# Attention with an exact top-32 and a mixture of experts: the selection's table of counts in PSUM, and the offset's bf16 source as three padded rows

## The chip, the core and the metric

The kernel is one program on one core of a Trainium2 chip. Its metric is the device time of one execution in microseconds, and lower is better. The core has a TensorE for matrix products (PE; its weight loads, PEld, are listed apart), a VectorE (DVE), a ScalarE (ACT), a GpSimd (POOL) and a queue engine (SP) that issues most of the transfers. SBUF is the on-chip working memory. PSUM, eight banks of 2 KB a partition, is where TensorE writes.

## The reference

```python
def _attn_ref(q, k, v):                       # 8 batches, 8 heads, 576 positions, 64 wide
    scores = scale * np.matmul(q, k.transpose(0, 1, 3, 2))
    kth = np.partition(scores, -top_k, axis=-1)[..., -top_k:-top_k + 1]     # top_k = 32
    mask = scores >= kth
    scores = np.where(mask, scores, -1000000000.0)
    ...softmax over each row...
    return np.matmul(attn, v)

def _moe_ref(x, expert_emb, tau, w1, w2):     # 4608 tokens of 512, 8 experts of 1024
    logits = xn @ en.T / tau                  # rows of x and of expert_emb, normalized
    expert_idx = np.argmax(logits, axis=1)
    out[mask] = gate_w[mask, None] * (np.maximum(x[mask] @ w1[e], 0.0) @ w2[e])
```

Each row of scores keeps its 32 largest entries before the softmax. The result goes through one expert per token, with the gate's probability as its weight.

## The kernel before, in words

The work falls into two stages. The first is the attention, with part of the expert work threaded through it; the second is the rest of the experts. The change touches the first alone.

The attention runs over 32 head units: a unit is one head of two batches (`NU` = 32). A unit has nine score tiles of 128 query rows by 576 keys (the last 64 rows of both batches share a tile), so there are 288 tiles. One loop (lines 919 to 1094) writes the program out step by step. Step i takes up a new tile on every engine, each engine at another point of the pipeline, and each engine runs its instructions in just this order. For one tile j the points are:

- step j-2: TensorE computes the scores into `sc` (`nat`, line 184), ScalarE copies them to SBUF as `xs` (line 663);
- steps j and j+1: VectorE finds the top eight of each of eight groups (line 670) and merges them (lines 680 to 686). The merge gives the maximum and a lower bound on the threshold;
- step j+2: ScalarE counts with a Sign how many scores lie under that bound (line 692), GpSimd multiplies `xs` with the signs (`y`, line 698), so that VectorE can find the next eight values below the bound;
- step j+3: VectorE takes these eight (line 706). Then comes the **select** (line 707): a table `win` of 18 constants is compared with the count, the entry that fits is multiplied with the sorted values, and the sum is the 32nd largest value, `tall`;
- step j+4: ScalarE makes the second Sign, `s2`, against `tall` (line 714);
- step j+5: VectorE makes the **offset** `r` = max(s2 x 2^60, row maximum), bf16 in and out (line 720). TensorE subtracts it from the recomputed, transposed scores (line 752), so that everything outside the top 32 vanishes in the exponential (line 753).

Nine steps after a unit's first tile its output begins. In each step TensorE runs the scores of tile i+2, then a **chunk** (transposed scores and offsets of 128 keys, line 752), then the **AV matmuls** (line 767) that multiply the weights of an earlier chunk with the values and accumulate in the PSUM tile `po`, and at times a segment of expert work (lines 422 and 431). Two of the nine steps of a unit are longer on TensorE: one has a chunk for both batches, one has two AV groups. Twice in a unit ScalarE copies the finished sums out of `po` to `ob` (line 785).

On VectorE a step's order is: the offset of tile i-5; then, interleaved, the groups of tile i, the merge of tile i-1, and at the end the maximum (line 706) and the select of tile i-3. All of the eight PSUM banks are taken: one for the expert work, two for `sc`, one for `po`, four for the chunks. `po` is 512 columns wide; the AV matmuls use the first 365.

The framework that builds the program puts in the waits, and keeps track of reads and writes by tile: an instruction that reads a tile waits for its last writer, and a writer for its last readers. It does this for the whole tile, whatever columns are used; for a PSUM tile it orders the reads of two engines too.

Of the kernel before, what the change touches and what calls it, by code (L numbers as in the profile page):

```python
# [12 lines left out]
BF16 = mybir.dt.bfloat16  # L13
I32 = mybir.dt.int32
AF = mybir.ActivationFunctionType
# [5 lines left out]
B, H, S, D = 8, 8, 576, 64  # L21
N, DM, E, F = B * S, H * D, 8, 1024
P = 128
# [25 lines left out]
def attn_moe_kernel(ctx: ExitStack, tc: tile.TileContext, qk, vb, vt, emb, tau, w1, w2, out):  # L49
    nc = tc.nc  # L50
# [27 lines left out]
    win = consts.tile([P, 9, 2], F32, name="win", tag="win")  # L78
# [448 lines left out]
    with ExitStack() as sx:  # L527
        bk = sx.enter_context(tc.tile_pool(name="bk", bufs=1, side="right"))
        wk = sx.enter_context(tc.tile_pool(name="wk", bufs=2, side="right"))
# [10 lines left out]
        tall = wa.tile([P, NU * 9], F32, name="tall", tag="tall", bufs=1)  # L540
        call = wa.tile([P, NU * 9], F32, name="call", tag="call", bufs=1)
        sc = ps_s.tile([P, 2, 512], F32, name="sc", tag="sc")
        po = ps_s.tile([P, 512], F32, name="po", tag="po")
# [2 lines left out]
                             start=(n == 0), stop=(n == WU - 1))  # L546
        pov = po[:, 0:5 * VW].rearrange("p (t e) -> p t e", t=5)

        NV = 2
        vts = []  # L550
        for i in range(NV):
# [102 lines left out]
        xss, cas, zs, s1s, y2s, s2s, cnt1 = ({} for _ in range(7))  # L654
# [46 lines left out]
        def select(i):  # L701
            z = zs.pop(i)
            y2, c1 = y2s.pop(i), cnt1.pop(i)
            jk = wa.tile([P, 9, 2], F32, name=f"jk{i}", tag="jk", bufs=2)
            return [
                lambda: nc.vector.max(out=z[:, 16:24], in_=y2),  # L706
                lambda: nc.vector.scalar_tensor_tensor(  # L707
                    jk, win, c1, z[:, 15:24, None].to_broadcast([P, 9, 2]),
                    op0=ALU.is_equal, op1=ALU.mult, accum_out=tall[:, i:i + 1]),
            ]  # L710

        def sign2(i):
            s2 = wk.tile([P, S], BF16, name=f"s2_{i}", tag="s2", bufs=2)
            nc.scalar.activation(s2, xss.pop(i), AF.Sign, bias=tall[:, i:i + 1], scale=-1.0,  # L714
                                 accum_out=call[:, i:i + 1])
            s2s[i] = s2

        def offset(i):
            r = wk.tile([P, S], BF16, name=f"r{i}", tag="r", bufs=14)
# [198 lines left out]
        i = -1  # L918
        while i < ntile + 12 or sideq or later or bankq or early or squares or wq or mo["seg"] \
# [87 lines left out]
            for u, b in norms:  # L1007
                if u % H == 0:
                    for j in ((0, 2), (1,))[b]:
                        xt[u // H][0][j] = xp.tile([P, (4, 4, 1)[j], DM], F32,  # L1010
                                                   name=f"x{u // H}_{j}", tag=f"x{j}",
                                                   bufs=1 + (j > 0))
# [32 lines left out]
            if i == ntile + 4:  # L1045
                nc.vector.tensor_scalar(tall, tall, TMIN, 0.0, op0=ALU.is_lt, op1=ALU.add,
                                        accum_out=bad[:, 0:1])
# [5 lines left out]
                                        accum_out=bad[:, 2:3])  # L1053
# [43 lines left out]
    with mx:  # L1097
        wl = mx.enter_context(tc.tile_pool(name="wl", bufs=1, reuse_waits="tile"))
        wk = mx.enter_context(tc.tile_pool(name="mwk", bufs=1, reuse_waits="tile"))
# [475 lines left out]
```

## Time and profile before

| | |
|---|---|
| three runs, us | 1456.82, 1464.04, 1464.93 (median 1464.04) |
| the profiled execution, us | 1470.54 |
| its span, first to last instruction, us | 1468.8 |
| busy share of the span | PE 91%, VectorE 81%, ScalarE 68%, GpSimd 55% |
| mean granted TensorE clock | 0.955 of full speed |
| first and last select (line 707) begin, us | 23.1 and 1042.7 |

The attention stage thus takes about 1020 us of the span, and 287 steps lie between the two selects. A busy share over the whole span hides that the engines' loads differ between the stages, so the views below are cut at 1044 us. "Idle before, releaser" in the groups says how long the engine stood idle directly in front of a group's instructions, and what ended that.

### The profile page before, as it was taken

The page shows a single profiled execution, that of the slowest core. Times are in us where ns is not written, and L with a number is a line of the kernel's source. Part 1 is how long each engine was busy: PE and PEld are TensorE (multiplying, and loading weights), DVE is VectorE, ACT ScalarE, POOL GpSimd, SP SyncE. Part 2 cuts the span into 40 slices and gives each one's busy share as a digit, 9 for nine tenths or more (in the row PEclk, how much of TensorE's full clock was granted, in tenths as well). Part 3 has the DMA queues.
Part 4 walks back from the last instruction along what each step waited for, and adds up shares of the span by engine and source line. Part 5 has one row for each costly group of instructions (what it writes and reads, how often), then busy time and mean ns, then how long its engine had stood idle before and what let it go on. Part 6 is the DMA issues. An engine that isn't in the chain of part 4 may idle for free. (4 is left out here: it accounts for less than half of the span.)

```text
span 1468.8 us, 39480 instructions
## 1 busy us (share of the span) xinstructions
PE 1343.6 (91%) x13463; PEld 1145.1 (78%) x13463; DVE 1186.7 (81%) x5992; ACT 995.5 (68%) x2175; POOL 809.0 (55%) x1164
## 2 busy tenths in 40 slices
PE   6898889889879999999999999998988799999997
PEld 4787778778768887787787778877787688888886
DVE  7999999999999999999999999999861434444140
ACT  5797879788777888888887879887731334444241
POOL 4575766667776676678767657864560212222111
PEclk6799999999999999999999999999999899999999
DMA  6365544354344556555564636471343514445120
GB/s 182 89 172 147 131 125 120 100 157 108 101 104 102 153 157 198 144 151 156 136 189 133 205 104 191 109 171 63 107 114 142 177 40 173 165 169 178 43 74 33
DMA packets 117761, 194.96 MB, mean 133 GB/s; under 512 B 59671, under 2 KB 59671, under 8 KB 117410
## 3 DMA queue, kind: packets, MB, share of 16 engines
q1 hardware_dynamic: 109218, 168.96, 41.4%
q0 software_dynamic: 8192, 22.07, 4.5%
q8 instruction: 129, 2.11, 0.6%
q14 instruction: 222, 1.82, 0.4%
HBM read 115.29 MB, written 20.87 MB: 93 GB/s over the span
## 5 line engine op out<-in xcount | busy, mean ns | idle before, releaser
L698 POOL TENSOR_TENSOR y<-xs,s 128x576 f32<-128x576 f32 x288 | 370.3, 1286 | 223.3 <-DVE ca L670 102.2
L670 DVE MAX8 ca<-xs 128x8 f32<-128x72 f32 x2304 | 476.1, 217 | 0.6 <-ACT xs L663 0.6
L752 PE MATMUL pt<-st 128*128 128x288 f32 (+1 forms) x1280 | 307.4, 327 | 0.0
L184 PE MATMUL sc<-st 128*128 128x288 f32 x1280 | 272.8, 341 | 36.4 <-ACT xs L663 31.7
L767 PE MATMUL po<-v,w 128*64 128x73 f32 (+1 forms) x5760 | 277.6, 236 | 2.8 <-issue 2.5
L767 PEld LDWEIGHTS po<-v,w 128*64 128x64 f32 (+1 forms) x5760 | 231.2, 139 | 55.7 <-issue 34.0
L692 ACT ACTIVATE s<-xs,z 128x576 bf16<-128x576 f32 x288 | 222.8, 774 | 55.3 <-DVE z L686 54.8
L184 PEld LDWEIGHTS sc<-st 128*128 128x128 f32 x1280 | 193.7, 199 | 83.6 <-ACT xs L663 43.8
L714 ACT ACTIVATE s<-xs,tall 128x576 bf16<-128x576 f32 x288 | 223.1, 775 | 29.1 <-DVE jk L707 28.7
L753 ACT ACTIVATE w<-pt 128x576 f32<-128x576 f32 x288 | 188.9, 656 | 76.0 <-PE pt L752 75.4
L706 DVE MAX8 z<-y 128x8 f32<-128x576 f32 x288 | 213.1, 740 | 6.1 <-POOL y L698 6.1
L752 PEld LDWEIGHTS pt<-st 128*128 128x128 f32 (+1 forms) x1280 | 198.2, 190 | 4.9 <-issue 1.0
L663 ACT COPY xs<-sc 128x576 f32<-128x576 f32 x288 | 181.4, 630 | 23.0 <-PE sc L184 21.8
L720 DVE TENSOR_SCALAR r<-s,mall 128x576 bf16<-128x576 bf16 x288 | 190.4, 661 | 4.6 <-ACT s L714 4.5
L752 PE MATMUL pt<-negi,r 128*128 128x128 bf16 (+4 forms) x1600 | 138.8, 213 | 45.9 <-DVE r L720 45.9
L752 PEld LDWEIGHTS <-r 128*128 128x128 bf16 (+1 forms) x1920 | 95.7, 101 | 78.9 <-DVE r L720 49.6
L594 POOL TENSOR_TENSOR lo<-lo,hi 128x202 fp32r<-128x202 f32 x186 | 118.0, 634 | 15.5
L357 POOL DMA_INDIRECT out_dram<-ys_w,wi x20 | 22.7, 1134 | 167.2 <-ACT ys_w L1160 62.3
L707 DVE SCALAR_TENSOR_TENSOR jk<-win,c,z 128x18 f32<-128x18 f32 x288 | 108.4, 376 | 0.1
L1141 PE MATMUL ph_w<-xTh,w 128*128 128x448 f32 (+3 forms) x384 | 96.5, 332 | 5.6 <-ACT w L483 2.6
L1156 PE MATMUL py_w<-w,hh 128*128 128x512 f32 x320 | 99.8, 393 | 0.8 <-ACT ys L1160 0.8
L592 POOL TENSOR_SCALAR hi<-lo 128x202 fp32r<-128x202 f32 x186 | 73.2, 393 | 45.5 <-DMA lo<-in_qk 40.1
(246 smaller groups left out, 2321.9 us busy)
## 6 DMA issues: line engine op xcount, KB each, us to landing
r<-in_w SPq DMA_DIRECT2D x128, 256.0 KB, 5.1
fr<-in_w SPq DMA_DIRECT2D x28, 1024.0 KB, 6.4
lo<-in_qk SPq DMA_DIRECT2D x31, 608.0 KB, 4.0
st<-hi SPq DMA_DIRECT2D x62, 288.0 KB, 5.2
st<-lo SPq DMA_DIRECT2D x62, 288.0 KB, 5.3
st<-hi SPq DMA_DIRECT2D x31, 304.0 KB, 3.4
st<-lo SPq DMA_DIRECT2D x31, 304.0 KB, 4.3
v<-in_v SPq DMA_DIRECT2D x32, 288.0 KB, 3.6
```

Of the source, the lines that this page charges most:

```text
L184: nc.tensor.matmul(sc[:, hf, :SH], qs[:, cols(b)], kk[:, b * S + hf * SH:b * S + (hf + 1) * SH], start=(n == 0), stop=(n == len(terms) - 1))
L594: nc.gpsimd.tensor_tensor(lo[:, c], lo[:, c].bitcast(F32), hi[:, c].bitcast(F32), ALU.subtract)
L663: nc.scalar.copy(xs.rearrange("p (a b) -> p a b", a=2), sc[:, :, :SH])
L670: return [lambda gi=gi: nc.vector.max(out=ca[:, 8 * gi:8 * gi + 8], in_=xs[:, gi * GW:(gi + 1) * GW]) for gi in range(G)]
L692: nc.scalar.activation(s1, xss[i], AF.Sign, bias=zs[i][:, 15:16], scale=-1.0, accum_out=c1)
L698: nc.gpsimd.tensor_tensor(y2, xss[i], s1s.pop(i), ALU.mult)
L706: lambda: nc.vector.max(out=z[:, 16:24], in_=y2),
L714: nc.scalar.activation(s2, xss.pop(i), AF.Sign, bias=tall[:, i:i + 1], scale=-1.0, accum_out=call[:, i:i + 1])
L720: nc.vector.tensor_scalar(r, s2s.pop(i), BIG, mall[:, i, 0:1], op0=ALU.mult, op1=ALU.max)
L752: nc.tensor.matmul(o_, l_, r_, start=(n == 0), stop=(n == len(seq) - 1))
L753: nc.scalar.activation(w.rearrange("p (a b) -> p a b", a=2), ps[:, :, :SH], AF.Exp, scale=0.125)
L767: nc.tensor.matmul(o, w[:, q:q + 64], vc, start=start and n < 2, stop=stop and n in (8, 7 - b))
```

## The change

```diff
         pov = po[:, 0:5 * VW].rearrange("p (t e) -> p t e", t=5)
 
+        winp = po[:, 400:418].rearrange("p (a b) -> p a b", a=9)
+        nc.vector.tensor_copy(winp, win)
+
...
                 lambda: nc.vector.scalar_tensor_tensor(
-                    jk, win, c1, z[:, 15:24, None].to_broadcast([P, 9, 2]),
+                    jk, winp, c1, z[:, 15:24, None].to_broadcast([P, 9, 2]),
                     op0=ALU.is_equal, op1=ALU.mult, accum_out=tall[:, i:i + 1]),
...
         def sign2(i):
-            s2 = wk.tile([P, S], BF16, name=f"s2_{i}", tag="s2", bufs=2)
-            nc.scalar.activation(s2, xss.pop(i), AF.Sign, bias=tall[:, i:i + 1], scale=-1.0,
-                                 accum_out=call[:, i:i + 1])
-            s2s[i] = s2
+            s2 = wk.tile([P, 3, S // 3 + 2], BF16, name=f"s2_{i}", tag="s2", bufs=2)
+            s2s[i] = s2[:, :, :S // 3]
+            nc.scalar.activation(s2s[i], xss.pop(i).rearrange("p (a b) -> p a b", a=3), AF.Sign,
+                                 bias=tall[:, i:i + 1], scale=-1.0, accum_out=call[:, i:i + 1])
```

The table of 18 constants is copied once into columns 400 to 417 of `po`, behind the columns of the AV matmuls. The select reads it there, so that one of its two tensors is in PSUM and one (the sorted values) in SBUF. The second Sign's output lies as three rows of 192 elements, 194 apart, and the offset reads these three rows and writes `r` as one run of 576, as before. What is computed stays the same.

As `po` is one tile for the framework, the select now takes part in its waits. On VectorE, around the select of tile 55 (the step in which TensorE also runs the AV matmuls of `w5_0_3`), the order before is:

```order
L670 MAX ca58_3822<-xs58_3704 128x8
L707 SCALAR_TENSOR_TENSOR jk55_3825,tall_165<-win_84,c1_55_3754,z55_3691 128x18 [waits DVE_49]
L720 TENSOR_SCALAR r54_3906<-s2_54_3831,mall_164 128x576 [waits PE_49,Activation_49]
L670 MAX ca59_3902<-xs59_3762 128x8
L680 MAX mall_164<-ca58_3822 128x8 [waits DVE_49]
```

and now, three lines further down in the source:

```order
L673 MAX ca58_3823<-xs58_3705 128x8
L710 SCALAR_TENSOR_TENSOR jk55_3826,tall_165<-po_168,c1_55_3755,z55_3692 128x18 [waits DVE_49,PE_49]
L723 TENSOR_SCALAR r54_3907<-s2_54_3832,mall_164 128x576 [waits Activation_49]
L673 MAX ca59_3903<-xs59_3763 128x8
L683 MAX mall_164<-ca58_3823 128x8 [waits DVE_49]
```

Nothing moved, but the select waits for TensorE: for the AV matmuls of its own step. Behind it, in VectorE's order, stand the next step's offset, groups and merge. On TensorE, the AV matmuls of that step and of the next one, `w5_0_4`, stood like this before:

```order
L767 MATMUL po_168<-v1_188,w5_0_3_3764 64x73 x9
L184 MATMUL sc_167<-st6_3219 128x288 [waits Activation_49]
L184 MATMUL sc_167<-st6_3219 128x288 x3
L752 MATMUL pt5_1_0_3920<-st5_2617 128x288 [waits Activation_49]
...
L767 MATMUL po_168<-v1_188,w5_0_4_3848 64x73 [waits Activation_49]
L767 MATMUL po_168<-v1_188,w5_0_4_3848 64x73 x8
```

and now:

```order
L770 MATMUL po_168<-v1_189,w5_0_3_3765 64x73 x9
L184 MATMUL sc_167<-st6_3220 128x288 [waits Activation_49]
L184 MATMUL sc_167<-st6_3220 128x288 x3
L755 MATMUL pt5_1_0_3921<-st5_2618 128x288 [waits Activation_49]
...
L770 MATMUL po_168<-v1_189,w5_0_4_3849 64x73 [waits DVE_49,Activation_49]
L770 MATMUL po_168<-v1_189,w5_0_4_3849 64x73 x8
```

The first AV matmul of a step waits for the select of the step before. In the whole program 281 of the 288 selects name TensorE among what they wait for, 158 first AV matmuls name VectorE (the others have waited for a later VectorE instruction already), and 62 of the 64 copies of `po` on ScalarE now wait for the select of the step before in place of TensorE.

## Rows read from the trace of the kernel before

**Rows 1.** The span in 40 equal slices of 36.7 us, on the page: each digit is the busy share in tenths, and PEclk the granted TensorE clock in tenths of full speed.

```profile
PE   6898889889879999999999999998988799999997
DVE  7999999999999999999999999999861434444140
PEclk6799999999999999999999999999999899999999
```

**Rows 2.** Windows: stretch in us and its length, then busy us (and instructions) of PE, PEld, DVE, ACT and POOL, the granted clock, the DMA share and GB/s.

```profile
20.00:325.00 305.00, 269.75 (x3212) 233.16 (x3210) 304.95 (x1687) 246.40 (x574) 196.93 (x294) 0.91 0.51 136
325.00:1044.00 719.00, 671.71 (x7907) 562.16 (x7908) 708.18 (x3922) 592.41 (x1330) 501.46 (x734) 0.97 0.51 137
460.00:520.00 60.00, 60.00 (x716) 49.74 (x716) 59.56 (x346) 52.00 (x115) 42.61 (x65) 1.00 0.51 135
1044.00:1468.80 424.80, 389.49 (x2308) 342.38 (x2304) 161.49 (x311) 147.35 (x258) 100.43 (x103) 0.97 0.36 122
```

**Rows 3.** Groups of VectorE's instructions by line and shape, whole span: count | busy us, mean ns of one | idle before.

```profile
L670 DVE MAX8 ca<-xs 128x8 f32<-128x72 f32 x2304 | 476.1, 217 | 0.6 <-ACT xs L663 0.6
L720 DVE TENSOR_SCALAR r<-s,mall 128x576 bf16<-128x576 bf16 x288 | 190.4, 661 | 4.6 <-ACT s L714 4.5
L707 DVE SCALAR_TENSOR_TENSOR jk<-win,c,z 128x18 f32<-128x18 f32 x288 | 108.4, 376 | 0.1
...
L484 DVE TENSOR_TENSOR w<-fr,w 128x512 fp32r<-128x512 f32 x56 | 37.9, 687 | 13.2 <-ACT w L483 12.8
L484 DVE TENSOR_TENSOR w<-fr,w 128x1024 fp32r<-128x1024 f32 x28 | 33.7, 1224 | 4.2 <-ACT w L483 3.7
...
L515 DVE TENSOR_TENSOR xTl<-px_w,xTh 128x512 fp32r<-128x512 f32 x24 | 15.9, 686 | 81.8 <-ACT xTh L514 81.8
...
L481 DVE CAST w<-r 128x1024 fp32r<-128x1024 f32 x2 | 1.4, 690 | 0.0
```

**Rows 4.** The same lines one by one: duration of one in ns as min/median/max, first and last start in us.

```profile
L707 DVE SCALAR_TENSOR_TENSOR jk<-win,c,z x288: 211/222/1348, 23.1 to 1042.7; 128x18 f32<-128x18 f32 x144
L720 DVE TENSOR_SCALAR r<-s,mall x288: 283/368/1459, 28.8 to 1044.2; 128x576 bf16<-128x576 bf16 x144
L706 DVE MAX8 z<-y x288: 730/741/762, 22.3 to 1041.9; 128x8 f32<-128x576 f32 x144
```

**Rows 5.** Timelines of GpSimd and of VectorE at two places: start us, us, engine, line.

```profile
205.42 1.28 POOL L698 TENSOR_TENSOR y<-xs,s 128x576 f32<-128x576 f32 x1 [1.58 <-DVE ca L670]
...
205.48 1.39 DVE L720 TENSOR_SCALAR r<-s,mall 128x576 bf16<-128x576 bf16 x1
...
475.82 0.62 POOL L796 TENSOR_TENSOR x<-ob,rd 128x256 f32<-128x256 f32 x1
...
476.02 0.45 DVE L707 SCALAR_TENSOR_TENSOR jk<-win,c,z 128x18 f32<-128x18 f32 x1
```

**Rows 6.** Who waited for whom between 20 and 1044 us: us in total, times, longest us.

```profile
PEld L752 <- DVE r L720: 49.6, 27, 2.8
PE pt L752 <- DVE r L720: 45.9, 26, 2.7
...
PE sc L184 <- ACT xs L663: 30.3, 31, 2.6
...
DVE z L706 <- POOL y L698: 6.1, 4, 2.8
```

**Rows 7.** Timelines of TensorE and of VectorE in the unit that begins near 200 us: AV matmuls (line 767), what follows them, and selects (line 707).

```profile
208.66 0.85 PE L767 MATMUL po<-v,w 128*64 128x73 f32 x18
...
209.31 0.22 DVE L707 SCALAR_TENSOR_TENSOR jk<-win,c,z 128x18 f32<-128x18 f32 x1
...
217.38 0.22 DVE L707 SCALAR_TENSOR_TENSOR jk<-win,c,z 128x18 f32<-128x18 f32 x1
...
217.61 1.48 PE L767 MATMUL po<-v,w 128*64 128x73 f32 x18
219.02 1.33 PE L184 MATMUL sc<-st 128*128 128x288 f32 x4
...
220.32 0.24 DVE L707 SCALAR_TENSOR_TENSOR jk<-win,c,z 128x18 f32<-128x18 f32 x1
...
223.30 1.00 DVE L707 SCALAR_TENSOR_TENSOR jk<-win,c,z 128x18 f32<-128x18 f32 x1
...
223.74 1.64 PE L767 MATMUL po<-v,w 128*64 128x73 f32 x36
```

**Rows 8.** Timeline of VectorE: two selects that lie 17 steps apart, and the gap in which the one-time copy of the table will stand.

```profile
8.65 0.18 DVE L66 COPY negt<-negi 64x64 bf16<-64x64 bf16 x1
10.81 0.36 DVE L628 TENSOR_TENSOR st<-x,st 64x192 fp32r<-64x192 f32 x1 [1.98 <-ACT st L627]
...
462.36 0.38 DVE L707 SCALAR_TENSOR_TENSOR jk<-win,c,z 128x18 f32<-128x18 f32 x1
...
519.79 0.22 DVE L707 SCALAR_TENSOR_TENSOR jk<-win,c,z 128x18 f32<-128x18 f32 x1
```

## The prediction

> **What bounds the kernel now.** I read the slices of the page first. VectorE is at 9 from the second slice to the 29th and falls off behind; TensorE stands at 8 and 9, and its granted clock is full in some slices of this stretch and below in others [rows 1]. So the stage that the change touches ends near 1044 us, and the windows are cut there. Between 20 and 1044 us VectorE is busy 304.95 + 708.18 = 1013.1 of 1024 us, 98.9%, and TensorE 269.75 + 671.71 = 941.5 [rows 2]. VectorE is the bound of this stage, with TensorE 8% behind; the last stage runs on TensorE and is not touched. The list of waits says the same: TensorE waits for the offset `r` (45.9 us, 26 times) and for scores that ScalarE has not copied (30.3), while VectorE hardly waits at all (6.1 for `y`) [rows 6].
>
> The reader should then look at what VectorE's time is made of. The groups give 661 ns for an offset and 376 for a select of only 18 elements [rows 3]. One by one, the select takes 222 ns in the median and 1348 at most, the offset 368 and 1459, while the maximum over 576 elements, with one source of 4-byte elements, stays between 730 and 762 [rows 4]. The two lines that the change touches are the ones that get held, and the timelines show by what: an offset that starts at 205.48, 0.06 us behind a GpSimd product of 1.28 us, takes 1.39 us, to 0.17 us after the product's end; a select at 476.02 takes 0.45 us and ends 0.03 us after the GpSimd product that began at 475.82 [rows 5]. So time goes to waiting for GpSimd inside an instruction, where no list of waits shows it.
>
> **The change part by part.** *The select from PSUM.* 288 selects at a mean of 376 ns; a free one takes 222 [rows 3, 4]. If reading the table from PSUM ends the holding, each gains 154 ns, together 44.4 us of VectorE. Bounds: nothing gained, and 376 - 211 = 165 ns (47.5 us). What a source in PSUM costs by itself is seen in a pair of rows: 128x512 with one source in PSUM (line 515) takes 686 ns, the same size from SBUF alone (line 484) 687 [rows 3]. I take no extra cost.
> [...]
>
> *The offset from three rows.* No instruction of the trace before has such a source, so I bound it. From 512 to 1024 elements line 484 grows by 537 ns: 1.05 ns an element, and 150 ns fixed. At line 481 a cast of 1024 elements takes 690, that is 0.53 ns an element; the shortest offset, 283 ns, leaves (283 - 150) / 576 = 0.23 [rows 3, 4]. [...] An offset then pays 576 x 0.26 = 151 ns more than now and is not held: 283 + 151 = 434 at least, 368 + 151 = 519 from the median, 454 by the cast's rate. I take 519, next to the offset's own median: 661 - 519 = 142 ns, 40.9 us over 288. The ends: 434 gains 65.4 us; with both doublings lost 754 by line 484's rate, and as much as 839 with the 85 ns that the median stands above the shortest, which loses 27 to 51 us.
>
> Together 44.4 + 40.9 = 85.3 us of VectorE. A tile costs VectorE (1013.1 - 85.3) / 288 = 3.22 us, other work included, against a pace of (1042.7 - 23.1) / 287 = 3.553 today [rows 4].
>
> *What is late next.* From 460 to 520 us TensorE is busy 60.00 of 60 us at full clock [rows 2], and 17 steps take 519.79 - 462.36 = 57.43 us, 3.378 each [rows 8]. That is TensorE's own pace where it also carries expert work, and VectorE's new 3.22 is below it. The window from 325 to 1044 us holds 719 / 3.553 = 202 steps; at 3.378 they take 683, a gain of 36 us, 11 above TensorE's busy time there. Before 325 us TensorE has less to do (269.75 of 305), and VectorE keeps the bound: 86 steps lose 86 x 0.296 = 25.5 us, if nothing new holds it.
>
> *The new waits.* The select waits for the AV matmuls of its own step, and behind it in VectorE's queue stand the next offset, groups and merge, for which TensorE and ScalarE wait. Where TensorE is ahead this is free: at 208.66 + 0.85 = 209.51 the matmuls end as the select of 209.31 runs. Where VectorE is ahead it costs: in the step with two chunks the select starts at 217.38 and the matmuls end at 217.61 + 1.48 = 219.09, 1.7 us later; at the step with two AV groups it is 223.30 against 225.38, 2.1 us, of which 1.7 are paid already [rows 7]. This is no loss where TensorE sets the pace: the next chunk needs the offset only after 1.33 us of scores and part of itself, and select plus offset take 0.22 + 0.52. In the early window I charge the middle of 0 and 1.7 us a unit, 0.85 x 9.5 units = 8 us. ScalarE's copies of `po` now wait for a select that is done a quarter of a microsecond after those matmuls; ScalarE is busy 838.8 of 1024 [rows 2], which covers it. TensorE's first AV matmul waits for the select before it: with 1.33 us of scores and a whole chunk between, I charge nothing.
>
> The rest costs nothing: the one-time copy stands in VectorE's gap between 8.83 and 10.81 us [rows 8]; ScalarE's second Sign writes as many elements as before.
>
> The sum: 36 + 25.5 - 8 = 53 us. The profiled execution took 1470.5, so 1417; it lies 6.5 us above the median of the runs, so I forecast 1411.
>
> **The rivals.** *The handshake gives it all back (slower).* VectorE and TensorE are tied in every step: neither may lead by more than a step's rest. If each unit pays VectorE's 2.1 us [rows 7] and TensorE also pays where VectorE is late (the select at 209.31 ends at 209.53, while AV matmuls of line 767 ran from 208.66; such a step would start them 0.9 us later), that is 3.0 x 32 = 96 us against 85: 1481, or 1475 on the scale of the median. It decides from 85.3 / 32 = 2.67 us a unit. For it speaks that both engines are near full and a unit's steps are uneven; against it, that a wait in one direction takes slack from the other, so the two seldom add up. At half this price or a little more the result is no change, about 1462.
>
> *The offset gets slower (slower).* If the three rows cost both doublings, or the offset is held as before and pays the 151 ns on top (812), the second part loses 27 to 51 us, the first gains 44, and the handshake at 1.7 x 32 = 54 is paid on a VectorE that is still the bound: 1507 to 1531, with the middle at 1519, or 1513 by the median. This includes the case that the change doesn't do what it says. [...]
> [...]
>
> *TensorE gets faster too.* In the early window its clock is 0.91, in the stretch without idle 1.00 [rows 2]. If the stage loses its gaps and the clock with them stays full, 941.5 x 0.95 = 894 us of TensorE bound it, and with VectorE at 928 and a little handshake it ends near 940: 84 us off, 1387, or 1380 by the median.
>
> **How the numbers follow.** The forecast of 1411 has 0.59 (its own range 1390 to 1440); a faster TensorE 0.10; the handshake at half price, near no change, 0.13; at full price 0.09; the slower offset 0.09. A measurement of this kernel tells 0.5%, 7 us, from no change. Faster by more than that: the first two, and a little of the third, 0.71. Within: 0.10. Slower: 0.19, with the upper end of the third. The range from 1378 to 1468 leaves out the dearest handshake and the slower offset above and little below.
>
> **What would show it.** In the changed profile the select should stand near 222 ns with a maximum of a few hundred, the offset near 519 with hardly any spread; a median near 750 would mean the plain rate, a maximum over 1.2 us that it is still held. VectorE's idle time before the select, put down to `po`, shows the handshake: under 40 us in sum or in places where TensorE has no gap fits the forecast. TensorE should be busy over 95% between 325 us and the stage's end, with its waits for `r` below 20 us. The forecast is wrong if VectorE and TensorE both stand idle more than 60 us in the stage.

## The result, and the profile after

| | before | after |
|---|---|---|
| runs of one comparison, median us | 1463.49 (4 runs, 1456.82 to 1464.93) | 1424.57 (4 runs, 1420.53 to 1432.68) |
| ratio, 95% interval | | 0.975 [0.971, 0.980] |
| the profiled execution, us | 1470.54 | 1420.53 |
| first and last select begin, us | 23.1 and 1042.7 | 21.5 and 995.2 |

The changed kernel is 2.5% faster. It was forecast at 1411 us, 13.6 below what came; the profiled execution, forecast at 1417, took 1420.53. The profiled execution before was slower than each of the four runs, and the one after is the fastest of its four, so what is added up from the traces below (50.0 us between them) overstates the 38.9 us between the medians. In the runs below, medians leave out one execution each of the kernel before, of the four rows and of two of the three with the AV matmuls first, which fell in a slower state. The lines moved down by three or four: the select is now line 710, the offset 723, its Sign 718, the AV matmuls 770.

The slices of the changed kernel's page, as in [rows 1], show the same picture some 48 us shorter: VectorE full up to the stage's end, now with the clock at 9 (90% or more) from the third slice on, but for one.

```profile
PE   6998999998989999999999999999979899999997
...
DVE  8999999999999999999999999999842224454240
...
PEclk6899999999999999999999999999998999999999
```

The windows, with the columns of [rows 2], cut at the new stage's end:

```profile
20.00:325.00 305.00, 279.20 (x3362) 240.91 (x3362) 298.78 (x1767) 261.04 (x600) 202.80 (x307) 0.94 0.53 142
325.00:997.00 672.00, 642.91 (x7770) 538.63 (x7769) 656.21 (x3834) 582.76 (x1302) 485.57 (x720) 1.00 0.53 144
997.00:1418.80 421.80, 386.52 (x2283) 339.77 (x2282) 160.56 (x310) 146.17 (x255) 100.27 (x102) 0.97 0.36 123
```

TensorE is busy 642.91 of 672 us behind 325 us, 95.7%; VectorE 97.7%. The second stage takes about what it took (424.8 us before, 421.8 now). So nearly all of the gain lies in the attention stage: its 287 steps take 3.393 us each instead of 3.553, a gain of 45.9 us from first to last select: 14.7 over the first 87 steps, 31.2 over the rest.

The changed instructions one by one, with the columns of [rows 4] (line 792 is a small fp32 operation of 5 or 10 elements, `rd`, which the change doesn't touch):

```profile
L710 DVE SCALAR_TENSOR_TENSOR jk<-po,c,z x288: 219/236/241, 21.5 to 995.2; 128x18 f32<-128x18 f32 x144
...
L710 DVEq EVENT_SEMAPHORE  x283: 21/21/1573, 21.4 to 994.8; - x142
...
L723 DVE TENSOR_SCALAR r<-s,mall x288: 432/508/515, 24.9 to 996.4; 128x576 bf16<-128x576 bf16 x144
...
L792 DVE TENSOR_SCALAR rd<-ob x36: 153/497/1159, 77.9 to 1012.7; 128x10 f32<-128x10 f32 x28, 128x5 f32<-128x5 f32 x8
```

and `rd` in the kernel before:

```profile
L789 DVE TENSOR_SCALAR rd<-ob x36: 145/166/1057, 85.3 to 1060.3; 128x10 f32<-128x10 f32 x28, 128x5 f32<-128x5 f32 x8
```

Neither the select nor the offset is held any longer: the maxima fell from 1348 and 1459 ns [rows 4] to 241 and 515. But the median of `rd` went from 166 to 497 ns: 27 of the 36 now take over 200 ns, against 17 before, and each of these ends within 0.2 us of a GpSimd instruction's end. And 283 of the 288 selects have a semaphore instruction of their own in VectorE's queue in front of them. In the three-row kernel below, whose select doesn't wait for TensorE, there are two.

Who waited for whom between 20 and 1000 us, with the columns of [rows 6]:

```profile
PEld L755 <- DVE r L723: 29.3, 33, 1.7
PE pt L755 <- DVE r L723: 24.4, 30, 1.6
...
ACT ob L788 <- DVE jk L710: 13.6, 41, 0.6
...
DVE jk L710 <- PE po L770: 12.5, 23, 1.5
PE po L770 <- DVE jk L710: 3.6, 6, 1.1
```

TensorE's waits for `r` fell by some 40% (44.8 and 41.3 before in the same window). The new rows are those between the select and `po`, in both directions.

What VectorE's time went to is best added up from start to start. An instruction's record can overlap the one before it (a select's by 81 ns at the median before, by 30 after), so I count each from its own start to the next one's, without the idle time between. From 20 us to the stage's end, us:

| | before | after |
|---|---|---|
| offset | 167.5 | 122.2 |
| select | 87.8 | 46.6 |
| MAX8 of the groups (2280) | 314.2 | 330.3 |
| `rd` | 8.6 | 16.0 |
| all of VectorE | 1013.8 | 955.2 |
| idle | 11.0 | 22.0 |

Offset and select give back 45.3 + 41.2 = 86.5 us, as forecast (85.3). Only 58.6 arrive in the sum, and 11 of these go to idle time. Two things stand against the saving: `rd`, now held more, with 7.4 us, and the MAX8, which cost 16.1 us more; the other 4.4 are spread over smaller groups. For the MAX8 the timeline shows where. Start us, us, engine, line:

```profile
600.93 0.22 DVE L673 MAX8 ca<-xs 128x8 f32<-128x72 f32 x1
601.12 0.24 DVE L710 SCALAR_TENSOR_TENSOR jk<-po,c,z 128x18 f32<-128x18 f32 x1
```

The select starts 0.19 us after the MAX8 in front of it, although nothing was waited for. With the table in SBUF it starts 0.14 us after (timeline of the three-row kernel below). Over all selects the gap between the end of that MAX8's record and the select's start has a median of -30 ns after and -81 before: some 51 ns of overlap are lost in each step.

### The profile page after: what moved, and what is told of

It reads as the page before. It is cut to its first block, busy times and chain, and to the rows that moved or that the text cites. A ratio compares the mean times of both kernels' runs of the same rounds, so it can differ in the third digit from the quotient of the medians.

```text
span 1418.8 us, 39624 instructions
## 1 busy us (share of the span) xinstructions
PE 1322.2 (93%) x13463; PEld 1128.0 (80%) x13463; DVE 1129.3 (80%) x5993; ACT 1000.1 (70%) x2175; POOL 800.2 (56%) x1164
## 5 line engine op out<-in xcount | busy, mean ns | idle before, releaser
L673 DVE MAX8 ca<-xs 128x8 f32<-128x72 f32 x2304 | 481.9, 220 | 0.7 <-ACT xs L666 0.7
L755 PE MATMUL pt<-st 128*128 128x288 f32 (+1 forms) x1280 | 301.3, 321 | 0.0
L184 PE MATMUL sc<-st 128*128 128x288 f32 x1280 | 268.6, 337 | 21.2 <-ACT xs L666 17.6
L770 PE MATMUL po<-v,w 128*64 128x73 f32 (+1 forms) x5760 | 271.5, 233 | 13.6 <-issue 5.0
L770 PEld LDWEIGHTS po<-v,w 128*64 128x64 f32 (+1 forms) x5760 | 226.3, 137 | 66.9 <-issue 33.7
L718 ACT ACTIVATE s<-xs,tall 128x576 bf16<-128x576 f32 x288 | 223.2, 775 | 32.9 <-DVE jk L710 30.6
L184 PEld LDWEIGHTS sc<-st 128*128 128x128 f32 x1280 | 189.8, 195 | 65.5 <-ACT xs L666 27.4
L755 PEld LDWEIGHTS pt<-st 128*128 128x128 f32 (+1 forms) x1280 | 193.6, 186 | 4.5 <-issue 1.0
L755 PE MATMUL pt<-negi,r 128*128 128x128 bf16 (+4 forms) x1600 | 137.3, 211 | 24.8 <-DVE r L723 24.4
L723 DVE TENSOR_SCALAR r<-s,mall 128x576 bf16<-128x576 bf16 x288 | 146.1, 507 | 0.5 <-ACT s L718 0.2
L755 PEld LDWEIGHTS <-r 128*128 128x128 bf16 (+1 forms) x1920 | 94.0, 99 | 57.5 <-DVE r L723 29.3
L357 POOL DMA_INDIRECT out_dram<-ys_w,wi x20 | 23.1, 1155 | 167.8 <-ACT ys_w L1163 64.1
L1126 PE MATMUL ph<-xTh,w 128*128 128x256 f32 x384 | 74.9, 294 | 12.3 <-issue 10.5
```

What stands on the lines that cost most here:

```text
L184: nc.tensor.matmul(sc[:, hf, :SH], qs[:, cols(b)], kk[:, b * S + hf * SH:b * S + (hf + 1) * SH], start=(n == 0), stop=(n == len(terms) - 1))
L673: return [lambda gi=gi: nc.vector.max(out=ca[:, 8 * gi:8 * gi + 8], in_=xs[:, gi * GW:(gi + 1) * GW]) for gi in range(G)]
L718: nc.scalar.activation(s2s[i], xss.pop(i).rearrange("p (a b) -> p a b", a=3), AF.Sign, bias=tall[:, i:i + 1], scale=-1.0, accum_out=call[: ...
L723: nc.vector.tensor_scalar(r, s2s.pop(i), BIG, mall[:, i, 0:1], op0=ALU.mult, op1=ALU.max)
L755: nc.tensor.matmul(o_, l_, r_, start=(n == 0), stop=(n == len(seq) - 1))
L770: nc.tensor.matmul(o, w[:, q:q + 64], vc, start=start and n < 2, stop=stop and n in (8, 7 - b))
```

## The experiments

All ratios are to the kernel before, in the same comparison (its median was between 1464.6 and 1465.5 us), with 95% intervals.

### One part at a time

**The table in PSUM alone.** The offset's source stays one run of 576.

```diff
-            s2 = wk.tile([P, 3, S // 3 + 2], BF16, ...)
-            s2s[i] = s2[:, :, :S // 3]
+            s2 = wk.tile([P, S], BF16, ...)
+            s2s[i] = s2
...
```

> Only the first half of the change: the table in PSUM, the offset's source as one run of 576. Theory: the select is free of GpSimd (236 ns, no spread) and gives VectorE 40 us back, but brings the handshake on po, which by the changed kernel's trace costs VectorE some 30 us (16 of lost overlap in front of the select, 14 of waits), and the offset is held as before (mean 660 ns or more, maximum over 1300), as what GpSimd no longer takes from the select it takes from the offset. Ratio to the kernel before 0.990 to 1.005. Rival, the select's part carries the gain: ratio 0.98 or below.

Measured: 1527.42 us, 1.045 [1.039, 1.051], slower by 63 us. Select and offset behave as expected; the time, expected at 0.990 to 1.005, does not. One by one:

```profile
L710 DVE SCALAR_TENSOR_TENSOR jk<-po,c,z x288: 223/236/241, 21.5 to 1092.0; 128x18 f32<-128x18 f32 x144
...
L723 DVE TENSOR_SCALAR r<-s,mall x288: 291/515/1484, 25.0 to 1093.2; 128x576 bf16<-128x576 bf16 x144
```

and what the select and the offset waited for and made wait, between 20 and 1000 us:

```profile
PEld L755 <- DVE r L723: 67.0, 36, 2.8
PE pt L755 <- DVE r L723: 61.9, 33, 2.6
...
DVE jk L710 <- PE po L770: 35.4, 45, 1.6
```

The select is freed just as in the whole change, and costs 41 us less. The offset behind it takes exactly that up: 208.8 us from start to start against 167.5, with 137 offsets over 600 ns against 83. On top come 17.6 us at the MAX8 and 35 us of idle time. Counted in the traces, of GpSimd's products `y` 65 held a select before and 73 an offset; here none and 132. So the time in which VectorE is held does not go away when the select is freed: the offset, directly behind it in the queue, takes it up.

**The three rows alone.** The table stays in SBUF.

```diff
...
-                    jk, winp, c1, z[:, 15:24, None].to_broadcast([P, 9, 2]),
+                    jk, win, c1, z[:, 15:24, None].to_broadcast([P, 9, 2]),
```

> Only the second half: the offset from three rows, the table in SBUF, no handshake. Theory: the offset takes 507 ns with no spread, the select is held more than before (mean 376 or more, since GpSimd's time is no longer spent on the offset), VectorE gets some 40 us back and TensorE, with fewer waits for r, lets most of it through: ratio 0.975 to 0.985, about the whole change's. Rival, both halves are needed since the held time only moves from one line to the other: ratio 0.99 to 1.00.

Measured: 1410.23 us, 0.964 [0.959, 0.969]: faster than the whole change by 14 us, and than the 0.975 to 0.985 expected. One by one:

```profile
L707 DVE SCALAR_TENSOR_TENSOR jk<-win,c,z x288: 216/228/1347, 21.8 to 979.9; 128x18 f32<-128x18 f32 x144
...
L707 DVEq EVENT_SEMAPHORE  x2: 21/21/21, 21.7 to 25.5; - x2
...
L720 DVE TENSOR_SCALAR r<-s,mall x288: 427/508/514, 27.5 to 981.2; 128x576 bf16<-128x576 bf16 x144
```

The place in front of the select:

```profile
600.55 0.22 DVE L670 MAX8 ca<-xs 128x8 f32<-128x72 f32 x1
600.69 0.23 DVE L707 SCALAR_TENSOR_TENSOR jk<-win,c,z 128x18 f32<-128x18 f32 x1
```

The offset is the same as in the whole change. The select is still held at times, with a mean of 330 ns, though less than the 376 of [rows 3], where the expectation had it held more. The held time of the offset did not pass on to the select: 43 products `y` hold one here, against 65 before, and behind the offset stand MAX8s, which are not held (before, one of 2304 took over 260 ns). VectorE's idle time in the stage is 3.6 us, and all but two selects have no semaphore instruction in front of them. Step for step it takes 3.338 us against 3.393 of the whole change. So the whole gain of the change, and more, is the rows'.

**The waits without the gain.** The rows alone, with the select's unused products (`jk`) written into `po` instead of SBUF; the table is read from SBUF, and is held as before.

```diff
-            jk = wa.tile([P, 9, 2], F32, name=f"jk{i}", tag="jk", bufs=2)
+            jk = po[:, 400:418].rearrange("p (a b) -> p a b", a=9)
```

> The handshake without its gain: rows_only, and the select (its table still in SBUF, so still held by GpSimd) writes its 18 unused products into columns 400 to 417 of po, so that it waits for the AV matmuls of its step and they for it. Theory, the handshake costs 15 to 30 us: ratio 0.010 to 0.020 above rows_only's. Rival, the handshake is free since TensorE sets the pace: the same ratio as rows_only.

Measured: 1520.98 us, 1.040 [1.035, 1.045], 111 us above the rows alone. The select and its waits:

```profile
L707 DVE SCALAR_TENSOR_TENSOR po<-win,c,z x288: 233/246/1379, 21.4 to 1089.5; 128x18 f32<-128x18 f32 x144
...
L707 DVEq EVENT_SEMAPHORE  x283: 21/21/1407, 21.3 to 1088.7; - x142
its engine sat idle before it (us, times) until:
  PE po L767: 27.8, 32
```

From the rows alone to this run VectorE's idle time in front of the select grows by 32 us, the lost overlap is (87 - 30) x 288 = 16 us, and the select's mean goes from 330 to 557 ns, 65 us: together 113. The waits alone thus cost 48 us, more than the 8 of the forecast, and the run lies 0.076 above the rows alone, where 0.010 to 0.020 was expected. Why the select is also held longer shows where GpSimd waits for the MAX8 in front of the select before it makes `y`. With the rows alone, and then in this run:

```profile
620.92 0.22 DVE L670 MAX8 ca<-xs 128x8 f32<-128x72 f32 x1
621.06 0.22 DVE L707 SCALAR_TENSOR_TENSOR jk<-win,c,z 128x18 f32<-128x18 f32 x1
621.15 1.28 POOL L698 TENSOR_TENSOR y<-xs,s 128x576 f32<-128x576 f32 x1 [0.24 <-DVE ca L670]
...
617.78 0.21 DVE L670 MAX8 ca<-xs 128x8 f32<-128x72 f32 x1
617.96 1.35 DVE L707 SCALAR_TENSOR_TENSOR po<-win,c,z 128x18 f32<-128x18 f32 x1
618.00 1.27 POOL L698 TENSOR_TENSOR y<-xs,s 128x576 f32<-128x576 f32 x1 [1.43 <-DVE ca L670]
```

The product starts 0.22 to 0.23 us after the MAX8 in both. With the rows alone the select starts 0.14 us after the MAX8, 0.09 ahead of the product, and runs through. Here it starts 0.18 after, 0.04 ahead, and is held to the product's end. In this run 70 products start less than 60 ns after a select, and 69 of these selects take over 1 us; with the rows alone it is 2 of 2. Where the product starts 70 to 200 ns after the select, none is held (36 selects here, 54 there). So the lost overlap of some 50 ns also loses the select its place ahead of GpSimd. The table in PSUM alone shows the same on the offset behind: 103 products start less than 60 ns after a select there (3 before), and 102 of them hold the offset.

**Four rows instead of three.** The whole change, with rows of 144.

```diff
-            s2 = wk.tile([P, 3, S // 3 + 2], BF16, ...)
+            s2 = wk.tile([P, 4, S // 4 + 2], BF16, ...)
...
```

> The whole change with four rows of 144 in place of three of 192, padded alike. Theory, the odd count is what keeps the offset from being held: with four rows the offset runs fast again (median 350 to 400 ns) and is held (maximum over 1200, mean over 600), and the time is that of psum_only. Rival, any layout in rows does it: offset near 507 ns without spread, ratio 0.975.

Measured: 1519.62 us, 1.037 [1.031, 1.044].

```profile
L723 DVE TENSOR_SCALAR r<-s,mall x288: 291/536/1480, 25.0 to 1094.1; 128x576 bf16<-128x576 bf16 x144
```

The offset is held again, with the same shortest duration as with one run of 576, and the time lies with that of the table in PSUM alone, as expected. So it is not the padding and not that the source comes in rows that frees the offset, but that there are three of them and not four.

### Where the price of the waits lies

**The wait moved to the MAX8 in front.** The whole change, but the MAX8 just before the select waits for the AV matmuls, so that the select waits for VectorE's own results alone, as before. 66 of the selects keep their semaphore instruction all the same.

```diff
...
+            if avs and len(ga) == G:
+                ga[-1] = lambda f=ga[-1]: tc.add_manual_dep(f().ins, last_av[0].name, ...)
```

> The whole change, with one wait moved: the MAX8 just before the select now carries the wait for TensorE's nine AV matmuls of this step, so that the select itself waits only for VectorE's own results, as in the kernel before. Theory (the handshake's price is in part overlap that is lost because the select carries a second wait: in the changed kernel the select starts 30 ns before the record of the MAX8 in front of it has ended at the median, with the table in SBUF 81 ns before): the gap in front of the select goes back to about -80 ns, 288 x 50 = 14 us come back, and the idle time for po (18 us) is found in front of that MAX8 instead; about 1406 to 1415 us, ratio 0.963 to 0.968. Rival (the overlap is lost through the PSUM operand, whatever the wait is carried by): no gain, 1420 to 1428, and the gap stays at -30 ns. Second rival: the MAX8 loses as much as the select gains, and the time is the changed kernel's.

Measured: 1415.85 us, 0.968 [0.964, 0.972]. One by one, the select, and what stood idle before it:

```profile
L710 DVE SCALAR_TENSOR_TENSOR jk<-po,c,z x288: 208/220/239, 21.6 to 997.2; 128x18 f32<-128x18 f32 x144
...
L710 DVEq EVENT_SEMAPHORE  x66: 21/21/331, 21.5 to 996.7; - x66
its engine sat idle before it (us, times) until:
  PE po L772: 0.9, 2
```

and the same place in a step, where nothing is waited for:

```profile
602.44 0.22 DVE L673 MAX8 ca<-xs 128x8 f32<-128x72 f32 x1
602.58 0.22 DVE L710 SCALAR_TENSOR_TENSOR jk<-po,c,z 128x18 f32<-128x18 f32 x1
```

The overlap is back: 0.14 us from MAX8 to select, a median gap of -83 ns, and a select of 220 ns with its table still in PSUM. So the overlap isn't lost by the source in PSUM but by the second semaphore that the select has to wait for. The two kinds of select in this one kernel say the same: the 66 with a semaphore instruction have a median gap of -32 ns and a record of 235, the other 222 have -83 and 219. Medians of gap and of start-to-next give -30 + 161 = 131 ns a select in the changed kernel and -83 + 144 = 61 here, 70 ns less, which would be 20 us over 288. From start to start the select and the MAX8 of the groups give back 18.0 us (46.6 + 330.3 against 42.3 + 316.6), but the MAX8 over `y2`, in front of the one that now waits, costs 7.0 more (197.3 against 190.3). The idle time remains and grows: 28.2 us of it now stand before the MAX8 that waits, and 29 there and before the select together, against 18.9. In the profiled executions the stage gains nothing by it (3.399 us a step against 3.393), but this one was the slowest of its seven, at 1423.62 us, with the others between 1414.83 and 1416.57. By the medians 8.7 us reach the time, at the upper edge of what was expected; the intervals of this and of the whole change just overlap, so this size is rough.

**AV matmuls ahead of the chunk on TensorE,** in the whole change, with the wait moved as above too, and with the rows alone as a control.

```diff
-            if main:
-                chunk(w_, (m9 > 4) * 1, (0, 1, 2, 3, 4, 0, 1, 2, 3)[m9])
             for x in avs:
                 av(*x)
+            if main:
+                chunk(w_, (m9 > 4) * 1, (0, 1, 2, 3, 4, 0, 1, 2, 3)[m9])
```

> The whole change, with TensorE's order inside a step changed: the nine AV matmuls come ahead of the score chunk that follows them in the changed kernel, so that their end, for which the select waits, comes earlier by the time of that chunk. Theory (the waits of VectorE for po, 18 us in the stage, come from AV matmuls queued behind other work on TensorE): VectorE's idle time for po falls under 6 us, 1406 to 1414 us, ratio 0.96 to 0.967. Rival (the AV matmuls now wait themselves for ScalarE's exponentials and hold up the chunk behind them): po's idle time falls, but TensorE's idle time grows by as much, 1420 to 1440.

> Both of the edits above in one kernel. If lost overlap (14 us) and idle time for po (12 to 18 us) are two separate prices of the handshake, they add up: 1395 to 1405 us, ratio 0.953 to 0.96, faster than the kernel with the rows alone (0.964). If both edits remove the same price, it stands where the better of them stands, and if TensorE has become the bound it stands at about 1400 whatever VectorE gains.

> Control: the three padded rows alone (the table of counts stays in SBUF), with the same reorder on TensorE. There is no wait of VectorE for po here, so the reorder has nothing to remove: 1405 to 1415 us, ratio 0.960 to 0.967, as the rows alone. If it is faster than that, the reorder helps for a reason of its own (scores ready earlier), and the gain of the AV order with the table in PSUM must be read against this one. If slower, the AV matmuls wait for ScalarE.

Measured: 1466.55 us, 1.002 [0.999, 1.005]; 1459.82, 0.998 [0.995, 1.002]; 1462.63, 0.999 [0.997, 1.002]. All three theories miss by 40 us and more, and the control shows that the order costs 52 us where VectorE doesn't wait for `po` at all. Its waits, between 20 and 1000 us:

```profile
ACT w L753 <- PE pt L752: 147.8, 183, 2.3
...
PEld po L767 <- ACT w L753: 26.7, 77, 0.5
PE po L767 <- ACT ob L785: 26.3, 34, 1.4
PEld po L767 <- ACT ob L785: 26.2, 27, 1.6
```

With the rows alone in the old order ScalarE waited 48.5 us for a chunk, here 147.8, and TensorE's AV matmuls, now with no chunk in front of them, wait for exponentials and for ScalarE's copies of `po`. That is what the rival of the first expectation names, though the time lies above its range too (1420 to 1440), and the waits for `po` on VectorE did not fall as it had them but grew (33.0 us in the first of the three, against 12.5).

**The select half a step later.** MAX8 over `y2` and select of a tile come right behind the next step's offset, and in the program ahead of that step's AV matmuls; once with the table in PSUM, once in SBUF.

```diff
-            gc = select(i - 3) if ok(i - 3) else []
+            gc = select(i - 4) if ok(i - 4) else []
...
             if ok(i - 5):
                 offset(i - 5)
+            for f in gc:
+                f()
```

> The whole change, with the select half a step later: the MAX8 over y2 and the select of a tile come one step later, right behind the offset at the head of VectorE's step, and stand in the program ahead of that step's AV matmuls. So the select waits for AV matmuls of the step before, which have long ended, and this step's AV matmuls wait for a select that is done some 1.2 us into the step. Theory (the handshake's price, 42 us against the rows alone, comes from where the select stands in the step, not from reading PSUM): VectorE's idle time for po falls under 4 us, the gap in front of the select is about -80 ns, VectorE's occupied time of the stage falls from 955 to about 935 us, and the time is 1385 to 1403 us, ratio 0.946 to 0.958, faster than the kernel with the rows alone (0.964). Rival (the wait only moves: ScalarE's second sign now waits for a select of the same step, and the offset of the next step for that sign): ACT's idle time for jk grows by more than 30 us and the time is 1415 us or more. Second rival: TensorE's AV matmuls wait for the select, 1405 to 1420.

> Control for the run before: the rows alone (table in SBUF), with the select at the same later place. It has no wait between VectorE and TensorE for po. Theory: the place itself gives nothing, 1405 to 1418 us, ratio 0.960 to 0.968, with the select still held by GpSimd (mean 300 to 400 ns); then the gain of the later select with the table in PSUM is the select's held time plus the handshake that is gone, 15 to 30 us between the two runs. Rival: the place changes what runs beside the select, and this control gains or loses more than 10 us by itself; then only the difference between the two runs tells of the table.

Measured: 1457.84 us, 0.995 [0.992, 0.998], and 1447.95, 0.990 [0.986, 0.994]. Both are far slower than expected. A first part is the rival of the first expectation: ScalarE's second Sign now waits for a select of the same step. In the kernel with the table in PSUM:

```profile
ACT s L718 <- DVE jk L710: 93.1, 168, 1.4
```

against 30.6 us in the whole change; with the table in SBUF it is 120.7 against 29.5. A second part neither expectation named. In the kernel with the table in PSUM:

```profile
599.30 0.75 DVE L709 MAX8 z<-y 128x8 f32<-128x576 f32 x1
600.15 0.23 DVE L710 SCALAR_TENSOR_TENSOR jk<-po,c,z 128x18 f32<-128x18 f32 x1
```

and in the other:

```profile
599.36 0.75 DVE L706 MAX8 z<-y 128x8 f32<-128x576 f32 x1
600.15 0.24 DVE L707 SCALAR_TENSOR_TENSOR jk<-win,c,z 128x18 f32<-128x18 f32 x1
```

The select now stands directly behind the MAX8 whose result it reads, and starts 104 ns (table in PSUM, with the second semaphore) or 35 ns (SBUF) after that record's end, where it starts 30 ns (whole change) or 87 ns (rows alone) before the end of the record in front at its old place. The old order had one other instruction between the two. From the end of the record in front to the next start a select takes 280 ns in the mean here against 210 in the whole change, and 261 against 172 with the table in SBUF: 20 of the 33 us lost, and 26 of the 38.

**The same, with one MAX8 of the groups between.**

```diff
-            for f in gc:
+            for f in gc[:1] + mix[:1] + gc[1:]:
                 f()
+            mix = mix[1:]
```

> The whole change with the later select, and one MAX8 over scores put between the MAX8 over y2 and the select, which reads that MAX8's result: with the two back to back the select started 104 ns after the record in front of it had ended, where it starts 30 ns before with work between. Theory (the back-to-back pair hid what the later place gives): the gap goes from +104 to about -80 ns, 288 x 184 ns = 53 us come back, about 1400 to 1410 us, ratio 0.955 to 0.963, and VectorE has next to no idle time for po. Then the later select with the table in PSUM is faster than the rows alone (0.964) or equal to them. Rival (the later place costs by itself, by ScalarE's second sign waiting for the select, 93 us with the pair back to back): 1420 to 1440, and ScalarE's idle time for jk stays above 80 us.

> Control for the run before: the rows alone with the same later select and the same MAX8 between. With the pair back to back the select started 35 ns after the record in front of it; with the MAX8 between it should start 81 ns before, 288 x 116 ns = 33 us, so about 1412 to 1420 us, ratio 0.964 to 0.970. Theory: the run with the table in PSUM is 5 to 25 us faster than this one, because there is nothing left of the handshake and the select is not held; that would show that reading the table in PSUM is worth its held time where no wait comes with it. Rival: this one is as fast or faster, as where the select stood before (1410 against 1425), and the table in PSUM loses for a reason other than the wait.

Measured: 1429.07 us, 0.977 [0.973, 0.980], and 1421.89, 0.971 [0.968, 0.975]. So the one MAX8 between gives 28.8 and 26.1 us. The first expectation's theory (1400 to 1410) fell, and its rival, that the later place costs by itself, has the time right: both kernels stay slower than with the select at its old place, by 4.5 and 11.7 us, and ScalarE's second Sign still waits 64.2 and 85.1 us for the select. The select with the table in PSUM:

```profile
L710 DVE SCALAR_TENSOR_TENSOR jk<-po,c,z x288: 213/236/240, 22.9 to 1002.9; 128x18 f32<-128x18 f32 x144
...
L710 DVEq EVENT_SEMAPHORE  x281: 21/21/21, 46.2 to 1002.8; - x141
its engine sat idle before it (us, times) until:
  PE po L770: 4.9, 11
```

and with the table in SBUF:

```profile
L707 DVE SCALAR_TENSOR_TENSOR jk<-win,c,z x288: 210/222/1226, 21.7 to 992.7; 128x18 f32<-128x18 f32 x144
```

At this place VectorE waits hardly at all for `po`, 7.4 us in all before the select, and the select in SBUF is held less (mean 291). The table in PSUM still loses: the second expectation's theory, 5 to 25 us in its favour, fell, and its rival held. From the end of the record in front to the next start a select takes 171 ns in the mean with PSUM, 145 without: 26 x 288 = 7.5 us, and the two times lie 7.2 apart. Where the waiting is gone, the second semaphore (median gap -30 against -82, record 236 against 222) costs almost as much as the holding, and the rest of the idle time decides.

The pairs, us, each with the same order of work:

| | table in SBUF | table in PSUM |
|---|---|---|
| offset from one run, select as before | 1464 | 1527 |
| three rows, select as before | 1410 | 1425 |
| three rows, select as before, wait on the MAX8 | 1410 | 1416 |
| three rows, AV matmuls first | 1463 | 1467 |
| three rows, AV matmuls first, wait on the MAX8 | 1463 | 1460 |
| three rows, later select, back to back | 1448 | 1458 |
| three rows, later select, one MAX8 between | 1422 | 1429 |

(With the table in SBUF there is no wait to move, so 1410 and 1463 stand twice.) Where the select itself waits, the table in PSUM loses in each pair, with the AV matmuls first by 4 us only, which is within the spread of its runs. Where the MAX8 carries the wait the difference is smaller, and with the AV matmuls first none is shown. The fastest kernel of the study, faster than both, is the one with the three rows alone.

## Why the prediction was right, and where it was not

The direction and the range were right; so was the bound (VectorE is at 9 up to the 28th slice, though, and not the 29th). One of the two parts did what was forecast, the other lost time where it was forecast to gain. Between the profiled executions the gain is 50.0 us for the 53 forecast, between the medians 38.9: most of the 13.6 us by which 1411 was missed is which executions were profiled.

**The offset at 519 ns, 40.9 us.** Right: 507 in the mean, never over 515, and 45.3 us from start to start. From one run and from four rows the offset is fast at its shortest (283 and 291 ns) and gets held (up to 1459 and 1480), from three rows it is neither (432 at the shortest). No run takes apart what three rows cost: the doublings of the rate, and the 0.26 ns an element (151 ns an offset) that the forecast charged, were the author's estimate. What the runs show in their place is 149 ns more at the shortest (283 to 432) and 140 in the median (368 to 508). Why three rows end the holding and four do not, no run shows either.

**The select at 222 ns, 44.4 us.** Right by itself: 41.2 from start to start. A cost of the source in PSUM does not show, as the forecast had it: the select takes 236 ns in the median, and 219 where it has one semaphore (the wait moved to the MAX8), against 222 with the table in SBUF before.

**The sum, 85.3 us of VectorE.** This step failed. The two savings arrived, but only 58.6 us of them in VectorE's sum. It took the held time of an instruction for its own, so that freeing each saves each. The runs show that it can pass on: from a freed select to the offset directly behind it (41 us, all of it, with the table in PSUM alone), and in the whole change to `rd` (7.4 us). The other way round, the freed offset made the select's held time smaller (87.8 to 73.9 us, rows alone), so that its own freeing was worth 27 us at this point, not 44. The larger part of the 28 us that are missing from the sum is not held time, though, but the 16.1 us at the MAX8, a price of the wait, which belongs to the next term.

**The handshake, 8 us.** The term that was most mis-sized. Against the rows alone VectorE pays 18.4 us more of idle time (18.9 in all in front of the select), 18.3 at the MAX8 of the groups, of which (87 - 30) x 288 = 16 are the overlap in front of the select, and 2.8 at `rd`; the select gives back 27.3 from start to start. With 3 us in smaller groups that is the 15 us by which the stage is longer. VectorE's waits were priced from timelines as idle time, and that was of the right order before 325 us (6.2 us). But two reasons failed: "no loss where TensorE sets the pace", for 12.8 us of the idle time lie behind 325 us, where a step takes 3.413 us against 3.376 with the rows alone; and, unsaid, that a wait costs nothing where nothing is waited for. A second semaphore cost the select some 70 ns every time (131 against 61 ns, above), and the order quoted ahead of the prediction showed it, as `[waits DVE_49,PE_49]` in place of `[waits DVE_49]`.

**What is late next, 3.378 us a step.** Nearly right: 3.413 behind 325 us, a gain of 31.2 for 36; before it 14.7 for 25.5 - 8 = 17.5. With the rows alone VectorE, busy 646.96 of the 650 us from 325 to 975, reaches 3.376 there; TensorE is busy 628.88, so that 3.378 is TensorE's own limit is not shown. TensorE is above 95% as forecast, its waits for `r` are 29.3 and 24.4 us and not below 20. The sum of 45.9 for 53 is close in part by luck: in the later window the forecast used only 3.553 - 3.378 = 0.175 us a step of the 0.296 that it gave VectorE, and this slack took in much of the lost 28 us.

**The rivals.** The handshake that gives it all back did not come about in the whole change, but losses of its size come with the table in PSUM alone and with the waits alone (1527 and 1521 us). Its mechanism, the waits, is real, with 48 us of the 111 in the latter; the rest there is time for which the select is held. The slower offset fell: 507 ns, never over 515, against its 754 and 812. TensorE's clock rose to 0.94 and 1.00 [rows 2 had 0.91 and 0.97], but not its pace beyond the forecast.

Not tried: a table in a PSUM bank that no other engine writes. All eight banks are taken, each by 512 fp32 columns of the kernel's tiles.

## What to carry to other kernels

Time that an instruction is held inside by another engine may pass on to the one behind it: before pricing its removal, list the instructions directly behind it that can be held too. Here freeing the select alone gave VectorE nothing, since the offset behind it was held in its place (41 us on both sides); freeing the offset alone (661 to 506 ns in the mean, 45 us over 288), with MAX8s behind it that were not held, gave all of its time and more: 54 us of the kernel's. A tensor put into another engine's tile buys its waits, and here each select that then waited for two semaphores started some 51 ns later against the record in front (median gap -30 against -81 ns), even where neither had to be waited for; a neighbour in the queue can carry one of them, at a price of its own (28.2 us of idle time in front of the MAX8 that did). And test a change of two parts by its parts: here one of them was a loss that the other covered.

## What the runs showed of the hardware

- A select that waits for two semaphores has an instruction of 21 ns in the queue ahead of it, and starts 51 to 57 ns later against the one in front (median gap -30 against -81 to -87 ns), with a record 14 ns longer (236 against 222). Within one kernel (the wait moved to the MAX8) it is -32 against -83 ns, and 235 against 219.
- A select directly behind the MAX8 whose result it reads starts 35 ns after that record's end; with one instruction between it starts 82 ns before the end of the record in front (the later select, table in SBUF): 117 ns. With a second semaphore as well (table in PSUM) it is 104 after and 30 before.
- A select with the table in SBUF is held to the end of a GpSimd product `y` that starts less than 60 ns after it (74 of 75 in the kernel before, the rows alone and the waits alone), and not held by one that starts 70 to 200 ns after it (150 of 150).
- An offset from a bf16 source of three rows of 192 takes 507 ns for 576 elements, never over 515; from four rows of 144 it takes 291 at the shortest and is held up to 1480.
- The fp32 operations of 5 and 10 elements, `rd`, are held as well: they have a median of 166 ns before and 497 after, up to 1159; all of them that took over 200 ns (17 before, 27 after) ended within 0.2 us of the end of a GpSimd instruction.
